# Attention and two feed-forward layers in one kernel: later first values, more buffers for queries and bias rows, a doubling copy in four pieces

## The chip, the cores and the metric

One core of a Trainium2 chip runs the whole program. The metric is the device time of one execution in microseconds (us). The engines named below are TensorE (PE: matmuls, with weight loads shown apart as PEld), VectorE (DVE), ScalarE (ACT), GpSimd (POOL) and SyncE (SP), whose queue issues nearly all DMA transfers of this kernel.

## The reference

Attention over 2 batches, 8 heads, 576 positions and head size 64, with a bias that a tiny network makes from the distance of the two positions; then two feed-forward layers of 1152 tokens, 512 wide, 2048 hidden.

```python
scores = scale * np.matmul(q, k.transpose(0, 1, 3, 2))
x = (psi_rel / psi_i)[..., None]          # log1p(|i-j|) / log1p(max(i,1))
bias = np.maximum(x @ w1 + b1, 0.0) @ w2  # 32 hidden units, 8 heads; the same for both batches
attn = softmax(scores + bias.transpose(2, 0, 1)[None])
x = matmul(attn, v)                       # to (1152, 512)
x = prelu(x @ w_in, alpha) @ w_out        # layer 1
return rational(x @ w_in2) @ w_out2       # layer 2: a cubic over 1 + |b0 h| + |b1| h^2
```

## The kernel before

**Blocks and steps.** The queries are cut in nine blocks (`BLOCKS`, line 36): row blocks 0 to 3 of 128 queries for each of the two batches, and a last block that holds the remaining 64 queries of both batches. A block has four steps of two heads, 36 steps in all. A step n has scores (L332, PE), the row maximum with the bias added (L344, DVE, which writes p), the exponential (L355, ACT), the flip of p by matmuls with the identity (L365 and L369, PE), its copies out (L375 and L379 on DVE, L381 on ACT), and the values (L393, PE).

**Bias blocks.** Both batches use one bias tile `bias[j]` for each row block j. It is made in eight rows (four for the last). A row has four hidden tiles h (L256 on ACT, L258 on DVE), eight matmuls (L272), an eviction into a tile be (L291 or L284 on ACT, L293 or L286 on DVE) and a move, a DMA from be into every eighth partition of the bias tile (`bias_move`, L298; L302 for the last block). The pool of be tiles has three buffers, so the eviction of row r waits until the move of row r-3 has landed. Row maxima of block 0 need all eight moves of bias block 0. The bias of the last block is made for 64 partitions, and `bias_again` (L306) copies it on DVE to the other 64, in two copies of four heads each.

**Loads.** SP issues, in order: the constants `sm`, the queries of block 0 (`load_q`, L219, 512 KB into a tile qraw), the keys by pairs of heads (`load_k`, L202, called K00 to K03 here for batch 0 and K10 to K13 for batch 1, 288 KB each), the second part of the table tt (L467), the values of a batch in five pieces (`load_v`, L213, 256 KB each). ACT casts a key tile (L206), DVE makes its low part (L210). The queries are cast on DVE (L237) and their low part made on POOL (L238, `split_q`). The pool `rq` has one qraw buffer: a load of queries waits until the last split of the block before is done. SP takes its instructions in order, so that what stands behind such a wait waits too.

**Order.** Nothing is scheduled by the compiler: `Agenda` (line 91) collects calls with a planned time and runs them sorted by it, so the numbers of table `Z` (line 72) set the order of each engine's instructions and nothing else. `warm` (L186) puts idle matmuls on PE at the start.

**After attention** come 96 up units (L686) and 96 down units (L701) of the feed-forward layers. Their weights are loaded by `unit_load` (L607, L609), and rebuilt on ACT (L617, L621), DVE (L625, L628, L650) and POOL (L655); the first of these run beside the last steps of attention, in the memory of the pools be, h and tt (`early_pools`).

Of the kernel before, what the change touches and what calls it, by code (L numbers as in the profile page):

```python
# [20 lines left out]
B, H, S, D = 2, 8, 576, 64  # L21
# [29 lines left out]
def row_tables():  # L51
# [36 lines left out]
}  # L88

# [16 lines left out]
def fused_kernel(ctx: ExitStack, tc: tile.TileContext, qT, q4T, kT, vp, m1_in, m1_out, m2_in, m2_out, small, ttab, out):  # L106
    nc = tc.nc
# [9 lines left out]
    ag = Agenda()  # L117
    pools = {}

    def open_pool(key, bufs, side, space=None):  # L120
        kw = {} if space is None else {"space": space}
        if space is not DRAM:
            kw["reuse_waits"] = "tile"
        cm = tc.tile_pool(name=key, bufs=bufs, side=side, **kw)
        pools[key] = (cm, cm.__enter__())
        return pools[key][1]
# [24 lines left out]
    pt_p = open_pool("pt", 2, "left")  # L151
    sm_p = open_pool("sm", 4, "left")
    xu_p = open_pool("xu", 1, "left")
    rq_p = open_pool("rq", 1, "left")
    q_p = open_pool("q", 8, "left")
    bb_p = open_pool("bb", 1, "left")
    ba_p = open_pool("ba", 1, "left")
    tt_p = open_pool("tt", 1, "right")
    h_p = open_pool("h", 10, "right")
    be_p = open_pool("be", 3, "right")  # L160
    ps_v = open_pool("ps_v", 1, "left", PSUM)
    ps_t = open_pool("ps_t", 2, "left", PSUM)
    ps_b = open_pool("ps_b", 1, "left", PSUM)
# [78 lines left out]
    bias, hid, bev, bps = {}, {}, {}, {}  # L242
# [60 lines left out]

    def bias_again(h):

        nc.vector.tensor_copy(out=bias[4][64:, h : h + 4], in_=bias[4][:64, h : h + 4])  # L306

    def bias_rows(j, r, at, step, at0, step0):
        z, z0 = step / 4.1, step0 / 4.1
# [166 lines left out]
    def step_time(n):  # L476
        t = T0
        for a, b, dt in ((0, 4, DT0), (4, 24, DT), (24, 32, DT2), (32, 99, DT3)):
            t += max(0, min(n, b) - a) * dt
        return t  # L480
# [12 lines left out]
    EARLY = rows[-1][2] + Z["bias_move"] * rows[-1][3] / 4.1 + 0.1  # L493
# [301 lines left out]
        nc.vector.memset(one, 1.0 + 1e-6)  # L795

    ag.at(step_time(20), moe_consts)
    ag.at(EARLY + 2.0, bias_again, 0)
    ag.at(EARLY + 4.0, bias_again, 4)
    ag.at(EARLY, early_pools)  # L800
    ag.at(M0 - 0.1, psum_u)
    ag.at(M1 - 0.1, late_psum)
# [123 lines left out]
```

## Time and profile before

| | us |
|---|---|
| median of 3 runs (lowest, highest) | 618.4 (617.63, 619.54) |
| the profiled execution | 615.66 |
| its span | 613.9 |
| PE busy | 595.5 (97%) |
| DVE busy | 519.8 (85%) |
| ACT busy | 436.6 (71%) |

The profiled execution is one more execution, with its own time: 1.76 us of it lie around the span. Times in the rows below are from the span's start. Busy time of PE says that matmuls were in it, not that they ran at the full clock; the granted clock is shown beside it as a share of 2.4 GHz.

### The profile page before, as it was taken

How to read it: one execution, taken by the hardware profiler on the slowest of the kernel's cores; microseconds unless marked ns; L12 is line 12 of the kernel's file. 1: busy time of each engine (PE TensorE's matmuls, PEld its weight loads, DVE VectorE, ACT ScalarE, POOL GpSimd, SP SyncE). 2: the span in 40 equal slices, each digit the busy share in tenths (PEclk: the TensorE clock that was granted, in tenths of full speed). 3: DMA queues.
4: the chain of work that ended last, by engine and by line, in shares of the span. 5: the costliest groups of instructions: out<-in, count | busy, mean ns of one | idle time of the engine just before them, and what ended most of it. 6: DMA issues, size and time to landing. Idle time of an engine off the chain costs nothing.

```text
span 613.9 us, 11091 instructions
## 1 busy us (share of the span) xinstructions
PE 595.5 (97%) x4278; PEld 522.0 (85%) x4278; DVE 519.8 (85%) x883; ACT 436.6 (71%) x724; POOL 77.1 (13%) x83
## 2 busy tenths in 40 slices
PE   8689999999999999999999999999999999999997
PEld 4456667767778999999999999998999999999985
DVE  6799898798688877779998787989999999789783
ACT  4789888889876555777766657787777887655660
POOL 1113222122235332000000020300000000000000
PEclk9889999999999999999999999999999999999999
DMA  9872444323553332445445557775200000001011
GB/s 248 187 198 76 117 118 119 97 72 94 151 152 104 94 113 105 137 130 157 156 146 168 172 167 234 204 253 188 87 1 0 1 2 0 2 0 52 1 52 52
DMA packets 41749, 67.62 MB, mean 110 GB/s; under 512 B 5040, under 2 KB 24800, under 8 KB 41696
## 3 DMA queue, kind: packets, MB, share of 16 engines
q1 hardware_dynamic: 41552, 66.57, 36.9%
q8 instruction: 33, 0.54, 0.4%
q10 hardware_dynamic: 144, 0.35, 0.2%
q14 instruction: 20, 0.16, 0.1%
HBM read 49.71 MB, written 6.58 MB: 92 GB/s over the span
## 4 chain that ended last, share of the span: by engine, by line
PE 78%; DVE 11%; DMA 5%; ACT 2%; issue 2%; POOL 0%; SPq 0%; DVEq 0%; ACTq 0%; POOLq 0%
PE ops L701 29%; PE hps L686 29%; PE bps L272 5%; PE pv L393 5%; PE s L332 4%; PE tp L369 4%; DMA bias<-be 2%; DMA qraw<-in_qT_dram 2%; DVE p L344 1%; DVE mid L625 1%; DVE h L258 1%; DVE w L655 1%; DVE ks L210 1%; DMA away<-mid 1%; DVE acc L773 1%
## 5 line engine op out<-in xcount | busy, mean ns | idle before, releaser
L686 PE MATMUL hps<-xh,w 128*128 128x384 f32 x768 | 204.0, 336 | 0.0
L686 PEld LDWEIGHTS hps<-xh,w 128*128 128x128 f32 x768 | 139.6, 188 | 1.1 <-issue 0.2
L686 PE MATMUL hps<-xl,w 128*128 128x384 f32 x384 | 128.7, 335 | 0.0
L701 PE MATMUL ops<-g,w 128*128 128x384 f32 x576 | 104.5, 336 | 0.0
L701 PE MATMUL ops<-w,g 128*128 128x512 f32 x432 | 102.5, 392 | 1.2 <-DVE acc L773 1.2
L701 PEld LDWEIGHTS ops<-g,w 128*128 128x128 f32 x576 | 100.8, 188 | 0.0
L701 PEld LDWEIGHTS ops<-w,g 128*128 128x128 f32 x432 | 80.7, 188 | 17.5 <-issue 1.5
L686 PEld LDWEIGHTS hps<-xl,w 128*128 128x128 f32 x384 | 72.1, 188 | 0.9
L756 ACT CAST g<-n 128x768 fp32r<-128x768 f32 x48 | 40.1, 835 | 40.0 <-DVE n L720 28.0
L355 ACT ACTIVATE p<-p,nm 128x576 f32<-128x576 f32 x72 | 55.7, 774 | 13.4 <-DVE nm L344 12.9
L272 PE MATMUL bps<-h,w2s 128*32 128x288 f32 x576 | 52.9, 432 | 8.9 <-DVE be L286 3.8
L625 DVE SCALAR_TENSOR_TENSOR mid<-mid,raw 128x512 int32<-128x512 int32 x64 | 48.9, 764 | 13.1 <-ACT mid L617 12.9
L258 DVE TENSOR_SCALAR h<-tt,sc,nb 128x576 f32<-128x576 f32 x98 | 55.8, 605 | 0.1
L344 DVE CUSTOM_DVE_ANT_0 p<-s,bias 128x576 f32<-128x576 f32 x72 | 52.3, 750 | 1.4 <-PE s L332 1.1
L761 DVE TENSOR_TENSOR g<-n,g 128x768 fp32r<-128x768 f32 x48 | 46.6, 970 | 7.8 <-ACT g L756 7.8
L332 PE MATMUL s<-ks,q 128*128 128x288 f32 x320 | 52.4, 308 | 0.6 <-DVE ks L210 0.6
L238 POOL TENSOR_TENSOR q<-qraw,q 128x256 fp32r<-128x256 f32 (+1 forms) x40 | 34.4, 859 | 144.2 <-DVE q L237 124.4
L628 DVE SCALAR_TENSOR_TENSOR mid<-raw,mid 128x512 int32<-128x512 int32 x64 | 49.5, 773 | 2.2
L369 PEld LDWEIGHTS tp<-ident,p 128*128 128x128 f32 x288 | 30.9, 141 | 23.5 <-issue 15.3
L393 PE MATMUL pv<-pt,v 128*64 128x128 f32 (+1 forms) x800 | 47.8, 267 | 0.2 <-DVE pt L375 0.2
L332 PEld LDWEIGHTS s<-ks,q 128*128 128x128 f32 x320 | 44.7, 192 | 2.6 <-issue 1.1
L369 PE MATMUL tp<-ident,p 128*128 128x128 f32 x288 | 46.6, 284 | 0.3 <-ACT pt L381 0.3
(77 smaller groups left out, 836.9 us busy)
## 6 DMA issues: line engine op xcount, KB each, us to landing
raw<-in_moe_w_in_dram SPq DMA_DIRECT2D x32, 512.0 KB, 4.3
raw<-in_moe_w_out_dram SPq DMA_DIRECT2D x32, 512.0 KB, 3.6
bias<-be SPq DMA_DIRECT2D x32, 288.0 KB, 4.8
qraw<-in_qT_dram SPq DMA_DIRECT2D x8, 512.0 KB, 5.5
away<-mid SPq DMA_DIRECT2D x16, 256.0 KB, 2.0
mid<-away SPq DMA_DIRECT2D x16, 256.0 KB, 3.9
v<-in_vp_dram SPq DMA_DIRECT2D x10, 256.0 KB, 7.5
kraw<-in_kT_dram SPq DMA_DIRECT2D x8, 288.0 KB, 5.0
```

Source lines behind the costliest of these rows:

```text
L258: nc.vector.tensor_scalar(out=h, in0=x, scalar1=sc[:, k : k + 1], scalar2=nb1, op0=ALU.mult, op1=ALU.max)
L272: nc.tensor.matmul(out=ps[32 * c : 32 * c + 32], lhsT=w2s, rhs=hid[j, r, c][:, u * HALF : (u + 1) * HALF], start=True, stop=True,)
L332: nc.tensor.matmul(out=ps[:, w, :HALF], lhsT=x[:, u, :], rhs=kk[:, h, w * HALF : (w + 1) * HALF], start=(i == 0), stop=(i == len(terms) - 1),)
L344: nc.vector.tensor_tensor_reduce(out=ptile[n][:, u, :].rearrange("p (w j) -> p w j", w=2), in0=pps.pop((n, u))[:, :, :HALF], in1=bias[j][: ...
L355: nc.scalar.activation(out=p, in_=p, func=AF.Exp, bias=nms.pop((n, u)), scale=-1.0, accum_out=sums[k][:, h : h + 1])
L369: nc.tensor.transpose(out=tp[:, j * P : (j + 1) * P], in_=p[:, u, o : o + P], identity=ident)
L393: nc.tensor.matmul(out=pv[64 * u : 64 * u + 64, hp, cols], lhsT=V[bb][:, j, h, :], rhs=pt[:, 4 * u + j if j < 4 else 8, cols], start=(j == ...
L625: nc.vector.scalar_tensor_tensor(out=m, in0=m, scalar=3, in1=raw[:, :, 0], op0=ALU.logical_shift_left, op1=ALU.bitwise_or)
L628: nc.vector.scalar_tensor_tensor(out=m, in0=raw[:, :, 1], scalar=-(2 ** 31), in1=m, op0=ALU.bitwise_and, op1=ALU.bitwise_or)
L686: nc.tensor.matmul(out=ps, lhsT=a, rhs=b, start=(i == 0), stop=(i == len(prs) - 1))
L701: nc.tensor.matmul(out=ops[ly, c, m], lhsT=a, rhs=b, start=(f == fs[0] and i == 0), stop=(f == fs[-1] and i == 2))
L761: nc.vector.tensor_tensor(out=gt[:, 1], in0=tmp.pop(p), in1=gt[:, 0].bitcast(F32), op=ALU.subtract)
```

## The change

The table of planned times: K02 and K03 are loaded at 9.5 and 11.2 instead of 3.0 and 3.2, the first values from 19.3 on instead of 4.0, and the next block's queries are loaded 2.6 after a block's first step instead of 5.34 (`loadq`).

```diff
-    "load_k00": 1.68, "load_k01": 1.9, "load_k02": 3.0, "load_k03": 3.2, "load_k10": 24.0,
+    "load_k00": 1.68, "load_k01": 1.9, "load_k02": 9.5, "load_k03": 11.2, "load_k10": 24.0,
...
-    rq_p = open_pool("rq", 1, "left")
+    rq_p = open_pool("rq", 2, "left")
...
-    be_p = open_pool("be", 3, "right")
+    be_p = open_pool("be", 4, "right")
...
     def bias_again(h):
 
-        nc.vector.tensor_copy(out=bias[4][64:, h : h + 4], in_=bias[4][:64, h : h + 4])
+        nc.vector.tensor_copy(out=bias[4][64:, h : h + 2], in_=bias[4][:64, h : h + 2])
...
-    ag.at(EARLY + 2.0, bias_again, 0)
-    ag.at(EARLY + 4.0, bias_again, 4)
+    for h in range(0, H, 2):
+        ag.at(step_time(29 + h // 2) + Z["again"], bias_again, h)
```

SP's queue at the program's start, before (kraw: keys, v_136: values of batch 0, bias<-be: the moves of the first bias block):

```order
L202 DMA kraw<-in_kT_dram 64x1152 x2
L467 DMA tt<-in_ttab_dram 128x472
L202 DMA kraw<-in_kT_dram 64x1152 x2
L213 DMA v_136<-in_vp_dram 128x512 x5
L298 DMA bias<-be 16x8x576 x8
L202 DMA kraw<-in_kT_dram 64x1152 x2
```

and the same place after the change:

```order
L202 DMA kraw<-in_kT_dram 64x1152 x2
L467 DMA tt<-in_ttab_dram 128x472
L298 DMA bias<-be 16x8x576 x2
L202 DMA kraw<-in_kT_dram 64x1152
L298 DMA bias<-be 16x8x576
L202 DMA kraw<-in_kT_dram 64x1152
L298 DMA bias<-be 16x8x576 x5
L213 DMA v_136<-in_vp_dram 128x512 x5
L202 DMA kraw<-in_kT_dram 64x1152
L219 DMA qraw<-in_qT_dram 128x1024
L202 DMA kraw<-in_kT_dram 64x1152
```

K02 and K03 now stand between the moves, and all five values behind the eighth; the queries of block 1 now go between K10 and K11.

DVE at steps 29 to 31, as the difference of the two (L306 is the doubling copy, L344 a row maximum, L237 a query cast):

```order
 L344 ISA nm 128x1
-L306 COPY bias<-bias 64x2304
-L237 CAST q<-qraw 128x256
-L306 COPY bias<-bias 64x2304
-L375 COPY pt<-tp 128x128
...
+L237 CAST q<-qraw 128x256
+L306 COPY bias<-bias 64x1152
 L379 COPY pt<-tp 128x512
 L375 COPY pt<-tp 128x128
```

The two long copies go; the first short one stands one step later, and the other three each a step further on, the last behind the row maxima of step 32.

## Rows read from the trace of the kernel before

**Rows 1.** The page: busy us of an engine, share of the span, instructions.
```profile
PE 595.5 (97%) x4278; PEld 522.0 (85%) x4278; DVE 519.8 (85%) x883; ACT 436.6 (71%) x724; POOL 77.1 (13%) x83
```
**Rows 2.** Busy us by engine in four stretches, granted clock, DMA share, GB/s.
```profile
30.00:38.00 8.00, 6.39 (x45) 3.94 (x45) 7.33 (x14) 5.94 (x12) 1.90 (x1) 0.79 0.56 145
80.00:160.00 80.00, 80.00 (x880) 56.97 (x880) 69.08 (x186) 69.61 (x146) 17.09 (x20) 1.00 0.40 108
170.00:175.00 5.00, 3.75 (x38) 2.93 (x38) 4.61 (x11) 2.24 (x5) 2.68 (x3) 1.00 0.19 64
175.50:190.30 14.80, 14.74 (x152) 12.85 (x151) 13.83 (x34) 11.93 (x26) 7.36 (x14) 1.00 0.51 143
```
**Rows 3.** Waits in the first 30 us: who waited for whom, total, times, longest.
```profile
ACT be L291 <- DMA bias<-be: 4.4, 1, 4.4
...
DVE be L293 <- DMA bias<-be: 3.8, 1, 3.8
...
PE bps L272 <- ACT be L291: 3.1, 1, 3.1
```
**Rows 4.** Timeline of SP's queue: start, us, issue, count.
```profile
4.68 4.85 SPq L213 DMA_DIRECT2D v<-in_vp_dram  x5
...
10.50 0.61 SPq L298 DMA_DIRECT2D bias<-be  x1
```
**Rows 5.** DMA issues of the first 30 us: count, KB, median us to landing.
```profile
bias<-be SPq DMA_DIRECT2D x8, 288.0 KB, 3.3
```
**Rows 6.** Stretches as in rows 2, where only keys, values, moves were on their way.
```profile
9.00:12.00 3.00, 2.95 (x33) 1.00 (x32) 3.00 (x7) 1.62 (x3) 0.00 (x0) 1.00 0.99 193
12.00:15.75 3.75, 3.51 (x36) 1.41 (x34) 3.46 (x8) 1.37 (x2) 0.00 (x0) 1.00 1.06 366
15.75:18.75 3.00, 0.17 (x3) 0.17 (x6) 0.00 (x0) 0.96 (x2) 0.00 (x0) 0.92 1.04 207
```
**Rows 7.** Timeline of DVE to the first row maximum; idle time before in brackets.
```profile
9.99 5.47 DVE L258 TENSOR_SCALAR h<-tt,sc,nb 128x576 f32<-128x576 f32 x11
...
20.01 3.51 DVE L258 TENSOR_SCALAR h<-tt,sc,nb 128x576 f32<-128x576 f32 x7
...
24.42 0.82 DVE L293 TENSOR_SCALAR be<-bps,cv 128x576 f32<-128x576 f32 x1 [0.70 <-PE bps L272]
25.27 2.65 DVE L210 TENSOR_TENSOR ks<-kraw,ks 64x1152 fp32r<-64x1152 f32 x2
...
28.14 1.48 DVE L258 TENSOR_SCALAR h<-tt,sc,nb 128x576 f32<-128x576 f32 x2
29.62 0.76 DVE L344 CUSTOM_DVE_ANT_0 p<-s,bias 128x576 f32<-128x576 f32 x1
```
**Rows 8.** Timeline of PE: the fifth bias row's matmuls, and the first values.
```profile
14.82 0.69 PE L272 MATMUL bps<-h,w2s 128*32 128x288 f32 x8
...
40.40 1.31 PE L393 MATMUL pv<-pt,v 128*64 128x128 f32 x20
```
**Rows 9.** Timeline of ACT: the first cast of batch 1's keys.
```profile
39.66 1.15 ACT L206 CAST ks<-kraw 64x1152 fp32r<-64x1152 f32 x1
```
**Rows 10.** Timeline near 66 us: DVE's cast of new queries, and PE's next wait.
```profile
66.10 0.29 DVE L237 CAST q<-qraw 128x256 fp32r<-128x256 f32 x1 [0.86 <-DMA qraw<-in_qT_dram]
...
66.88 0.69 PE L272 MATMUL bps<-h,w2s 128*32 128x288 f32 x8 [0.24 <-DVE be L286]
```
**Rows 11.** Timeline near the end of attention.
```profile
169.03 1.35 DVE L306 COPY bias<-bias 64x2304 f32<-64x2304 f32 x1 [0.62 <-DMA bias<-be]
...
174.50 0.33 PE L365 MATMUL tp<-ident,p 128*128 128x128 f32 x1 [1.02 <-ACT pt L381]
...
180.40 1.29 POOL L455 TENSOR_TENSOR xl<-xu,xh 128x512 fp32r<-128x512 f32 x1
...
180.69 1.53 DVE L650 CAST w<-mid 128x512 fp32r<-128x512 f32 x1
...
191.58 0.42 DVE L650 CAST w<-mid 128x512 fp32r<-128x512 f32 x1
```

4 rows, old and new, of the table Z are left out of this document.

## The prediction

> **What bounds the kernel now.** I read the page first: PE is busy for 97% of the span [rows 1], so time can only be won where PE has gaps, and the slices of the page put these in the first 70 us and near 170 us. The windows then say what limits each stretch. From 80 to 160 us PE is busy 80.00 of 80.00 us while DVE has some 11 us to spare [rows 2]: what happens there on DVE, ACT or in the queues costs nothing as long as it stays inside that slack, and a lead gained earlier is carried through. At 170 to 175 us PE is idle for 1.25 us [rows 2], of which the timeline shows 1.02 in one wait for ACT's copy out behind a late row maximum [rows 11]. After 200 us PE has the feed-forward layers alone, so the start and the end of attention move the finish one for one.
>
> At the start the list of waits names one event: ACT's eviction waited 4.4 us and DVE's 3.8 us for a move to land, and PE 3.1 us behind ACT [rows 3]. SP's timeline tells why. The five pieces of values were issued from 4.68 us on, the first move at 10.50 [rows 4], and what the queue has issued goes in order: the windows show keys on their way at 193 GB/s from 9 to 12 us, values at 366 from 12 to 15.75, and the first two moves at 207 from 15.75 to 18.75 [rows 6]. The rows of DVE give what follows: eleven h tiles end at 15.46, and after the wait its chain runs with only 0.70 us of idle time (for PE) to the first row maximum at 29.62 [rows 7].
>
> **The first values behind the moves, with four be buffers.** Removed: the values' 1.31 MB at 366 GB/s, 3.6 us ahead of the first move, and the two keys, 0.59 MB at 193, 3.1 us [rows 6]. Also the fifth eviction, not the fourth, is now the first that needs a move landed.
>
> What DVE could then do: PE has the fifth row's matmuls done at 14.82 + 0.69 = 15.51 [rows 8]. That eviction would start there instead of at 19.27 (15.46 and the 3.8 us of [rows 3]), 3.8 us earlier; without the 0.70 us for PE, whose chain loses its wait too, the eighth eviction would start at about 20.0, and the row maximum 29.62 - 24.42 = 5.2 us behind it [rows 7], at 25.2. That is 4.4 us earlier and the upper bound of this part.
>
> What the DMA can do: a lone move lands 3.3 us after issue [rows 5], so the first lands at 13.8, in time for 15.5. The others come as fast as the rows are made, one in about 1.4 to 1.9 us, and K02 and K03 are now among them. A move of 0.295 MB takes 1.43 us at 207 GB/s and a key 1.53 us at 193 [rows 6]. Ten transfers back to back: the fourth move lands at 13.8 + 3 x 1.43 + 2 x 1.53 = 21.1, the eighth at 21.1 + 4 x 1.43 = 26.9. The eighth eviction, which needs the fourth move's buffer, then starts at 21.1 and not 20.0; by DVE's chain the row maximum could start at 26.3, but needs the eighth move at 26.9. I take 26.9: a gain of 2.7 us. The lower bound is 20% slower transfers (13.1 us become 15.7, the eighth at 29.5): no gain in this part. I stay near the measured rates, since the moves and keys in the rows are the same instructions.
>
> From 30 to 66 us DVE sets the pace, with nearly every microsecond busy (7.33 of 8.00 at its start [rows 2]), and it issues the same list as before, so the 2.7 us are carried to PE's unbroken stretch.
>
> Cover for the moved loads: the values are through 3.6 us behind the eighth move, at 30.5, and the first values matmul, at 40.40 before, comes at 37.7 [rows 8]: 7 us to spare. Behind them K10 is through at 32.0; its cast, at 39.66 before [rows 9], comes at 37.0. Two keys and the queries of block 1 follow, and later moves stand behind these on SP, but their block is due only after 60 us. So I cost the late values at nothing; with that cover gone every microsecond of lateness would stop PE.
>
> **Two query buffers, loads at 2.6.** DVE waited 0.86 us for queries at 66 us and PE 0.24 us behind it [rows 10]. The wait goes, as the load no longer needs the last split. PE gets back only its 0.24 us. Elsewhere the query waits lie in stretches where PE is full, so nothing. The earlier load now stands ahead of the round trip of the inverse sums on SP; that trip is read by DVE several microseconds later and PE is full meanwhile. I cost it at nothing, at most the 11 us of DVE's slack hides it.
>
> **The doubling copies.** Two copies of 1.35 us each, with 0.62 us of waiting for the moves before the first, pushed the row maxima and made the 1.25 us of idle PE [rows 2, 11]. They go from there; four copies of half the size, some 0.70 us each, come. The first still lies before 175.5 us; three lie in the stretch 175.50 to 190.30, where DVE is busy 13.83 of 14.80 us and so has 0.97 us to give [rows 2]. Three copies are 2.1 us: DVE ends that stretch 2.1 - 0.97 = 1.1 us later against a start that is 1.25 us earlier. What is late next is thus the row maxima of the last block's steps. Gain 0.1 us; the bounds are 1.25 (all copies in gaps) and a loss worked out with the third rival.
>
> **Sum.** 2.7 + 0.24 + 0.1 = 3.0 us. Against the profiled execution: 615.66 becomes 612.7. That execution is 2.7 us under the median of the three runs, 618.4, and the prediction is for such a median: 618.4 - 3.0 = 615.4, or 0.5% less.
>
> **Rivals.** First, the DMA does not hold the moves back: the ten transfers overlap with the making of rows and the clock of DVE decides. For it: the first keys go while the fourth row is made. Against it: rows 6 show the transfers at these rates with the engines full. It gives 4.4 + 0.24, with up to 1.25 at the end 5.9 us: 612.5. (The page "DMA: Bandwidth & Descriptors" of the Trainium skill, section Specifications, has a ceiling of 435 GB/s towards SBUF, by which a move would take about 0.7 us, an estimate from that page, and this rival would hold; the trace has 207 GB/s and does not agree for moves of this shape.)
>
> Second, the stall comes back as a slow clock. PE runs out of work while the first row maximum is awaited; in 30 to 38 us it had a mean granted clock of 0.79, between its two levels of 1.2 and 2.4 GHz, after such a wait [rows 2]. Its keys and fifth to eighth bias rows now end earlier, so it may sit idle longer. If all of that stretch ran at 1.2 GHz, its 6.39 us would become 6.39 x 0.79 / 0.5 = 10.1; of the 3.7 us more, 1.6 fit in PE's idle time there, and 2.1 are lost. Then 1.0 us is left: 617.4. Against it: before, PE already lay idle 3.1 us at 15.5, and that goes.
>
> Third, and slower than before: the short copies meet POOL. When POOL was in a subtraction of 1.29 us from 180.40 to 181.69, DVE's cast of 180.69 took 1.53 us; the same cast took 0.42 at 191.58 [rows 11]. It ended about 0.4 us after POOL did. POOL is busy 7.36 of 14.80 us there [rows 2]. If each of the four copies waits out a whole subtraction, they cost 4 x (0.70 + 1.29) = 8.0 us; less 0.97 of slack and 1.25 of earlier start, the end of attention is 5.8 us later, and with the 2.9 gained before it the kernel is 2.8 us slower: 621.2. It turns to a loss when the copies' waits add up to more than 2.9 + 0.97 + 1.25 - 2.8 = 2.3 us, 0.6 each. Against it: only one of the copies follows a query cast that has just started POOL in that stretch. (The Trainium skill, "SBUF — State Buffer", section SBUF: two separate sides, says that VectorE and GpSimd share a port pair as an exclusive lock and the one that starts second waits for the whole instruction; the 1.53 us agree.)
>
> **How the numbers follow.** Forecast 0.58, with a range of its own of 613.6 to 616.8; first rival 0.17, second 0.17, third 0.08. A measurement of this kernel tells a change from none at about 0.3%, 1.9 us. Faster: nearly all of the forecast (0.54), the first rival and a little of the second (0.01): 0.72. Within 0.3%: the rest of both, 0.20. Slower: the third, 0.08. The range 612.3 to 618.5 takes in the first two rivals and the run-to-run spread of the median; the third lies outside.
>
> **What would show it.** Right: ACT's and DVE's waits for a move under 1.5 us in the first 30 us, the first row maximum near 26.9, waiting for the move and not for DVE; PE without a gap from about 63 us; the L393 matmuls of step 0 without a wait for values; 1.02 us of idle PE at 174 gone but DVE full to 190 and small PE waits near 188. First rival: row maximum near 25. Second: granted clock under 0.7 in the 8 us around it. Third: copies of over 1.5 us. The prediction is wrong if the shift at the first row maximum is not found again at 80 us, or if the end of attention gives back over 1 us.

## The result and the profile after

The change takes 612.88 us in the median of 4 executions (612.56 to 613.58), the kernel before, on the same chip, 618.97 (4 executions, 617.63 to 619.71): a ratio of 0.991 with an interval of 0.988 to 0.993. Timed once more, beside four of the experiments below, it is 612.96 (7 executions, 612.33 to 613.79) against 616.76 (13, 614.98 to 621.80), a ratio of 0.992 (0.989 to 0.995). So it is faster, by 3.8 to 6.1 us where 3.0 were forecast; 612.9 lies inside the range of 612.3 to 618.5, near its lower end, and below the 613.6 that the forecast alone would have allowed. The profiled execution of the change took 613.58 us, its span is 611.8; that is only 2.1 less than before. Profile and timing thus give different sizes, which is taken up further down.

The page's first part answers to [rows 1]; PE's share has not moved, since its busy time fell by 1.7 us where the span fell by 2.1:

```profile
PE 593.8 (97%) x4278; PEld 521.0 (85%) x4278; DVE 520.2 (85%) x885; ACT 437.0 (71%) x724; POOL 77.1 (13%) x83
```

DVE has two copies more. The waits of the first 30 us answer to [rows 3] (who waited for whom, total, times, longest):

```profile
DVE be L293 <- DMA bias<-be: 2.0, 1, 2.0
...
DVE p L344 <- DMA v<-in_vp_dram: 1.2, 1, 1.2
```

ACT no longer waits for a move. Two waits of DVE for moves are left. The second is a row maximum, which reads moves and no values; the profile names values, which were issued right behind the last move, but in the version with the values later (below) it names a move. SP's timeline (start, us, issue, count) answers to [rows 4], DVE's to [rows 7]. For DVE two more rows of before are needed, the first and the fifth eviction:

```profile
9.26 0.82 DVE L293 TENSOR_SCALAR be<-bps,cv 128x576 f32<-128x576 f32 x1
...
19.27 0.82 DVE L293 TENSOR_SCALAR be<-bps,cv 128x576 f32<-128x576 f32 x1 [3.81 <-DMA bias<-be]
```

After the change, SP and then DVE:

```profile
10.10 1.39 SPq L298 DMA_DIRECT2D bias<-be  x2
11.54 0.61 SPq L202 DMA_DIRECT2D kraw<-in_kT_dram  x1
12.64 0.54 SPq L298 DMA_DIRECT2D bias<-be  x1
13.22 0.60 SPq L202 DMA_DIRECT2D kraw<-in_kT_dram  x1
14.08 9.32 SPq L298 DMA_DIRECT2D bias<-be  x5
23.46 2.56 SPq L213 DMA_DIRECT2D v<-in_vp_dram  x5
```

```profile
9.26 0.82 DVE L293 TENSOR_SCALAR be<-bps,cv 128x576 f32<-128x576 f32 x1
9.98 5.48 DVE L258 TENSOR_SCALAR h<-tt,sc,nb 128x576 f32<-128x576 f32 x11
15.60 0.82 DVE L293 TENSOR_SCALAR be<-bps,cv 128x576 f32<-128x576 f32 x1
...
22.03 0.82 DVE L293 TENSOR_SCALAR be<-bps,cv 128x576 f32<-128x576 f32 x1 [1.98 <-DMA bias<-be]
...
28.38 0.76 DVE L344 CUSTOM_DVE_ANT_0 p<-s,bias 128x576 f32<-128x576 f32 x1 [1.18 <-DMA v<-in_vp_dram]
```

The fifth eviction starts at 15.60, where before it waited for a move until 19.27. The eighth waits 1.98 us for the fourth move (issued at 14.08, with two keys before it in the queue), and the first row maximum 1.18 us for the eighth move: it starts at 28.38, 1.24 us earlier than the 29.62 of [rows 7], and not 2.7. Then two pieces of PE's timeline, and windows with busy us by engine, granted clock, DMA share and GB/s (as [rows 2]):

```profile
24.38 1.29 PE L332 MATMUL s<-ks,q 128*128 128x288 f32 x8 [2.78 <-DVE ks L210]
...
30.30 1.19 PE L272 MATMUL bps<-h,w2s 128*32 128x288 f32 x8 [3.57 <-DVE be L286]
```

```profile
22.00:26.00 4.00, 1.62 (x12) 1.57 (x12) 3.93 (x5) 3.84 (x5) 0.12 (x1) 1.00 0.97 202
26.00:30.00 4.00, 0.73 (x9) 0.16 (x8) 2.82 (x7) 0.82 (x3) 0.88 (x1) 0.99 1.02 326
30.00:34.00 4.00, 3.70 (x24) 2.30 (x24) 3.85 (x7) 2.87 (x7) 1.90 (x1) 0.58 1.03 247
34.00:38.00 4.00, 3.94 (x37) 2.35 (x33) 3.64 (x7) 2.87 (x7) 0.00 (x0) 1.00 0.93 172
...
80.00:160.00 80.00, 80.00 (x889) 56.64 (x882) 68.22 (x185) 69.70 (x147) 17.84 (x21) 1.00 0.37 102
```

PE lies idle for 2.78 us until DVE has made the low part of a key, which stands behind the late eighth eviction, then for 3.57 us until DVE, done with the late row maximum, evicts the next bias row. In the 4 us after that its granted clock is 0.58, most of the time the lower of its two levels, 1.2 GHz. (Before, PE lay idle 3.07 us until 18.59, which is gone, and 2.06 in the place of the 3.57.) From 80 to 160 us PE is full, as before.

For all that follows two marks of the PE timeline are enough: the first scores of step 28, in the stretch where PE is full, and the first up matmul of the feed-forward layers. Before, then the change:

```profile
165.93 1.30 PE L332 MATMUL s<-ks,q 128*128 128x288 f32 x8
...
200.80 0.42 PE L686 MATMUL hps<-xh,w 128*128 128x384 f32 x1
```

```profile
164.22 1.31 PE L332 MATMUL s<-ks,q 128*128 128x288 f32 x8
...
199.10 0.42 PE L686 MATMUL hps<-xh,w 128*128 128x384 f32 x1
```

The lead is 1.24 us at the first row maximum, 1.71 at step 28 and 1.70 at the up matmul: what the start gave is carried on, and the end of attention (34.87 us from mark to mark before, 34.88 after) gives and takes nothing. From the up matmul to the end of the span it is 413.1 and 412.7 us.

### The profile page after: what moved, and what is told of

Its sections match the earlier page's. It is cut to its first block, busy times and chain, and to the rows that moved or that the text cites. A ratio compares the mean times of both kernels' runs of the same rounds, so it can differ in the third digit from the quotient of the medians.

```text
span 611.8 us, 11090 instructions
## 1 busy us (share of the span) xinstructions
PE 593.8 (97%) x4278; PEld 521.0 (85%) x4278; DVE 520.2 (85%) x885; ACT 437.0 (71%) x724; POOL 77.1 (13%) x83
## 4 chain that ended last, share of the span: by engine, by line
PE 80%; DVE 11%; DMA 4%; ACT 2%; issue 2%; SPq 0%; DVEq 0%; ACTq 0%
PE ops L701 29%; PE hps L686 29%; PE pv L393 6%; PE tp L369 5%; PE s L332 5%; PE bps L272 5%; DVE ks L210 1%; DVE h L258 1%; DMA bias<-be 1%; DVE p L344 1%; DVE mid L625 1%; DMA qraw<-in_qT_dram 1%; DVE w L655 1%; DMA away<-mid 1%; DMA v<-in_vp_dram 1%
## 5 line engine op out<-in xcount | busy, mean ns | idle before, releaser
L272 PE MATMUL bps<-h,w2s 128*32 128x288 f32 x576 | 51.3, 421 | 6.4 <-DVE be L286 5.1
L344 DVE CUSTOM_DVE_ANT_0 p<-s,bias 128x576 f32<-128x576 f32 x72 | 52.3, 751 | 2.8 <-PE s L332 1.3
```

Of the source, the lines that this page charges most:

```text
L272: nc.tensor.matmul(out=ps[32 * c : 32 * c + 32], lhsT=w2s, rhs=hid[j, r, c][:, u * HALF : (u + 1) * HALF], start=True, stop=True,)
L344: nc.vector.tensor_tensor_reduce(out=ptile[n][:, u, :].rearrange("p (w j) -> p w j", w=2), in0=pps.pop((n, u))[:, :, :HALF], in1=bias[j][: ...
```

## The experiments

One more event has to be known first: the first eviction of bias block 0 starts between 8.2 and 10.3 us after the span's start in the profiles, whatever the kernel. So the start of the first row maximum is also given relative to it: +20.4 before (29.62 - 9.26), +19.1 after (28.38 - 9.26).

**The kernel before, and the change, once more.** No edit.

> The kernel before, unchanged, for a second profile and for its spread. Measured so far: this change takes 5.8 us off (ratio 0.9906), but the two profiled executions differ by only 2.1 us (615.66 and 613.58), and the profiled one of before was 2 to 4 us quicker than all four timed ones. Theory A (the start): executions of before differ at the start, where a wait of 3 us cools PE; a second profile of 617 to 620 us shows the scores of steps 15 to 20 later by 2 to 4 us than in the first profile, with a lower granted clock between 15 and 45 us. Rival B (the end): the same lead up to 160 us, and the extra 2 to 4 us between 160 and 200. Rival C: spread evenly over the feed-forward layers. If the profile is again near 615.7, the three stay apart only by the clocks and times of the timed runs.

Measured: 616.40 us (12 executions), ratio 0.999 (0.997 to 1.000); row maximum at 29.14, +20.1; step 28 at 165.40. A second profile of the same program thus repeats the relative mark to 0.2 us and the other two to 0.5. It was again a quick execution, so it does not tell where the slower ones lose their time.

> The changed kernel, unchanged, on the same chip and in the same rounds as the three below. The kernel before had a median of 618.97 us over 4 runs beside its first timing and 616.77 over 29 runs since, so if the first four were on the high side the ratio here is 0.993 to 0.995 and not 0.9906; if the 5.8 us were real, 0.989 to 0.992.

Measured: 612.96, given above, 3.8 us under the kernel before and not 5.8; row maximum at 27.99, +18.7, after a wait of 0.53; yet step 28 came at 164.43, 0.21 us later than in the first profile. The windows of this profile say where 0.6 us went:

```profile
26.00:30.00 4.00, 2.12 (x17) 0.91 (x19) 3.47 (x9) 1.24 (x4) 0.99 (x1) 0.50 0.98 311
30.00:34.00 4.00, 4.00 (x24) 2.26 (x24) 3.46 (x6) 2.88 (x6) 1.90 (x1) 0.50 1.02 249
34.00:38.00 4.00, 4.00 (x33) 2.14 (x29) 3.43 (x6) 2.27 (x6) 0.00 (x0) 0.77 0.96 179
```

A clock of 0.50, 0.50 and 0.77 is the lower level for some 10 of these 12 us (4 + 4 + 4 x 0.23 / 0.5); in the first profile it was some 3.4 (4 x 0.42 / 0.5), and the earlier start is gone again. Here the clock was at the lower level before the second gap, from about 25.6 us on, behind a first gap of 2.98 us (2.78 in the first profile).

**The loads alone.** The kernel before with the three new load times.

```diff
-"load_k02": 3.0, "load_k03": 3.2, ... "load_v0": 4.0
+"load_k02": 9.5, "load_k03": 11.2, ... "load_v0": 19.3
```

> Before, with only the order of the first loads changed (values behind the moves, two keys among them): three be buffers, one query buffer, two long copies. Theory A: most of the gain is here: 2 to 4 us under before (ratio 0.9935 to 0.997); the fourth eviction needs the first move, landed at about 13.8, and waits about 0.5 us; the eighth needs the fifth move and waits about 1.5 us more than in the changed kernel. Rival B (the end of attention carries the gain): under 1 us (ratio above 0.998).

Measured: 614.87 (12), ratio 0.996 (0.994 to 0.998). ACT still waits 4.2 us for moves, DVE 3.5:

```profile
ACT be L291 <- DMA bias<-be: 4.2, 3, 2.6
...
DVE be L293 <- DMA bias<-be: 3.5, 1, 3.5
```

Row maximum at 28.62, +19.4. With three be tiles the later evictions take over the stall.

**The fourth be tile alone.** The kernel before with one number changed.

```diff
-    be_p = open_pool("be", 3, "right")
+    be_p = open_pool("be", 4, "right")
```

> Before, with only the fourth be buffer; values still ahead of the moves. The first move still lands near 17.7, so the fifth eviction (not the fourth) waits from 15.5 to about 17.8, and ACT's fourth not at all; the fourth move is issued near 14.3 instead of 18.6, so the back-to-back queue lands it at about 21.9 and the eighth eviction starts at 22 instead of 24.4. First row maximum near 27.7, 1.5 to 2 us earlier than in before; 614.8 to 615.8 us. Rival: the buffer only pays behind early moves; under 0.7 us gain.

Measured: 615.54 (12), ratio 0.9972 (0.9950 to 0.9995). DVE's timeline:

```profile
17.76 0.82 DVE L293 TENSOR_SCALAR be<-bps,cv 128x576 f32<-128x576 f32 x1 [2.64 <-DMA bias<-be]
...
28.64 0.76 DVE L344 CUSTOM_DVE_ANT_0 p<-s,bias 128x576 f32<-128x576 f32 x1
```

The fifth eviction still waits 2.64 us for the first move, which is behind the values, as expected. But the eighth starts at 23.46 and not at 22, after 1.26 us of waiting for PE, and the row maximum lies at +19.7; 1.5 to 2 us were expected from it. Against +20.1 to +20.4 before, the buffer gives 0.4 to 0.6, the loads 0.7 to 1.0, both 1.0 to 1.7 (the change): they add up. By the medians the two parts are worth 1.6 and 1.9 us, together 3.5, and 3.3 in the version with all but the queries: they add up too, but to about twice what the marks show, and where the rest is won stays open.

**All but the queries.** The change with `rq` at one buffer and `loadq` at 5.34.

> The change without its query part: one qraw buffer, queries loaded 5.34 after a block's first step. Prediction on record: 0.24 us of the gain, so the ratio to before within 0.001 of the change's 0.9906. Rival B: the query waits of before matter at the end (the queries of the last block came late, at 179.65), so 1 to 2 us of the gain are lost (ratio 0.992 to 0.994).

Measured: 613.50 (12, 612.73 to 617.92), ratio 0.996 (0.994 to 0.998). DVE's waits for queries from 60 to 200 us, in all 2.4 us, are back; the change has none. Both expectations gave a ratio (0.991, or 0.992 to 0.994) below the one measured; by the medians the version lies 0.5 us above the change, and its executions scatter up to 617.92 where those of the change end at 613.79.

**The queries alone.** The kernel before with those two numbers changed the other way.

> Before, with only the query part of the change: two qraw buffers, loads at 2.6. On record: 0.24 us. By the medians of the parts undone so far (613.50 without the queries, 612.96 with): 0.5 us, 616.2. Theory Q: the single buffer is what scatters the executions of before (615 to 621 us, with the profiled one always at the low end), since the kernels with two buffers lay within 2 us of each other and the two with one did not: then no execution here over 618 and a median of 615 to 616. Rival: scatter as before, and the two-buffer kernels were steady for another reason (the first wait for a move, which they all lack).

Measured: 615.54 (12, 614.88 to 616.51) against 617.17 (23, 615.37 to 622.37), ratio 0.997 (0.996 to 0.999). The forecast had 0.24 us for this part; the median gives 1.6. Its profile, at 615.45 us, has step 28 at 165.96, where before had 165.93. That is not to say that nothing was won, because its first row maximum came late:

```profile
30.59 0.76 DVE L344 CUSTOM_DVE_ANT_0 p<-s,bias 128x576 f32<-128x576 f32 x1
```

That is +21.9, and 1.0 to 1.5 us later than in the two profiles of before, though up to there the loads and moves are issued in the same order. The fifth eviction waited until 19.97 us for the second move (19.27 and 18.79 before), and the eighth 0.97 us for PE (0.70 and 0.72). From the row maximum to step 28 it is then 135.4 us, against 136.3 in both profiles of before: 0.9 us less, more than the forecast. Whether the query part won them or a late start was made up in slack, one profile does not tell. The spread changes too: a standard deviation of 0.52 us and nothing above 616.51, while a quarter of the executions of the kernel before, over all its timings, lie above 618 us.

**The long copies back.** The change with the old two copies.

```diff
-    for h in range(0, H, 2):
-        ag.at(step_time(29 + h // 2) + Z["again"], bias_again, h)
+    ag.at(EARLY + 2.0, bias_again, 0)
+    ag.at(EARLY + 4.0, bias_again, 4)
```

> The change with the two long doubling copies at their old places. Prediction on record: 0.1 us of the gain, so the same time as the change to 0.3 us, with a wait of PE near 172 back and the waits near 178 to 191 gone. Rival B: the short copies brought 1 to 2 us (ratio 0.992 to 0.994). Rival D: they cost time, since the lead of 3.5 us over before at step 30 is down to 2.1 at the end of attention: this kernel is 0.5 to 1.5 us faster than the change (ratio 0.988 to 0.990).

Measured: 612.99 (6), ratio 0.993 (0.991 to 0.996): by the medians the same as the change, 612.96 (the kernel before took 616.8 beside both), so that the four pieces are worth nothing. In its profile the wait of PE is back, and the end of attention takes 35.92 us instead of 34.88:

```profile
173.16 0.33 PE L365 MATMUL tp<-ident,p 128*128 128x128 f32 x1 [1.02 <-ACT pt L381]
...
170.00:175.00 5.00, 3.27 (x25) 2.61 (x21) 3.95 (x10) 3.23 (x8) 2.30 (x3) 0.85 0.71 217
175.00:180.00 5.00, 5.00 (x51) 4.19 (x50) 3.51 (x10) 3.44 (x8) 1.38 (x4) 0.81 0.24 71
```

The granted clock falls behind this wait, to 0.62 from 173 to 177.5 us, which neither profile of the kernel before shows there (1.00 from 165 to 200, with the same wait). This execution, 614.43 us, was the longest of the six. The kernel before has 34.87 us with the same copies. So the wait behind the long copies shows no cost in the medians, and 1 us in the one profile in which the clock falls behind it.

**Values later still.** The change with `"load_v0": 26.5` instead of 19.3, so that K10, the queries of block 1 and K11 stand between the last moves and the values.

> The change with the first values moved three transfers further back, behind K10, the queries of block 1 and K11. Theory F: what is behind the eighth move does not matter; it lands at about 28.3 as in the change, and the time is the same within 0.3%. Rival G: the eighth move, issued at 22.87, lands at 26 to 27 and the row maximum starts 1.2 us earlier, at the end of DVE's own chain (27.2).

Measured: 612.64 (6), ratio 0.991 (0.988 to 0.995). Row maximum at 26.92 after 0.60 us of waiting, now for the move; but the first eviction lay at 8.41, and +18.5 is 0.2 to 0.6 earlier than the change's two profiles, which differ by 0.45 themselves. So it is not seen that the values behind the moves hold the eighth one. What an empty queue behind it would do was not tried.

**Keys back to the front.** The change with K02 and K03 loaded ahead of all moves, as before.

```diff
-"load_k02": 9.5, "load_k03": 11.2
+"load_k02": 3.0, "load_k03": 3.2
```

> The change with keys K02 and K03 back ahead of the moves, where the queue has nothing to do from about 9 to 11 us; values still behind the moves. Theory F (ten transfers back to back, as on record): the fourth move lands near 18.5 instead of 21.9, DVE's wait of 2.0 us for it goes, the eighth eviction starts near 20.1, and the first row maximum at 25.2 to 26 instead of 28.4; 1 to 2.5 us faster than the change. Rival G (the eighth move is held by the values behind it, which is what the wait of 1.2 us is put down to): the row maximum comes only 2 us earlier, still after a wait for a landing. Rival H (DVE's lead at the start is eaten by PE's cold clock or by ACT before 66 us): row maximum 2 to 3 us earlier, the same total within 0.5 us.

Measured: 610.35 (6, 609.62 to 611.38), ratio 0.988 (0.985 to 0.991): 2.6 us better than the change, beside which it was timed, and no execution of the one reaches the other's. DVE's timeline has no wait for any move:

```profile
10.32 0.82 DVE L293 TENSOR_SCALAR be<-bps,cv 128x576 f32<-128x576 f32 x1
...
16.67 0.82 DVE L293 TENSOR_SCALAR be<-bps,cv 128x576 f32<-128x576 f32 x1
...
21.04 0.81 DVE L293 TENSOR_SCALAR be<-bps,cv 128x576 f32<-128x576 f32 x1
...
26.12 0.74 DVE L344 CUSTOM_DVE_ANT_0 p<-s,bias 128x576 f32<-128x576 f32 x1
```

Relative to the first eviction the row maximum comes at +15.8, 3.3 us earlier than in the change's first profile, and put on the 9.26 of the kernel before that gives 25.1: the 25.2 that the prediction had worked out as the bound by DVE's own chain. The clock after it:

```profile
26.00:30.00 4.00, 1.96 (x20) 1.34 (x24) 3.94 (x9) 4.00 (x8) 1.74 (x1) 1.00 0.97 299
30.00:34.00 4.00, 3.06 (x32) 1.72 (x32) 3.94 (x7) 2.18 (x5) 0.17 (x1) 1.00 1.02 234
34.00:38.00 4.00, 3.71 (x45) 2.35 (x44) 4.00 (x11) 3.70 (x6) 0.00 (x0) 1.00 1.03 197
```

PE's gap ahead of the first bias matmuls is 2.18 us here and the clock stays at 1.00. Step 28 and the up matmul:

```profile
161.49 1.30 PE L332 MATMUL s<-ks,q 128*128 128x288 f32 x8
...
196.45 0.42 PE L686 MATMUL hps<-xh,w 128*128 128x384 f32 x1
```

So the two keys between the moves cost the change 2.7 us at step 28. That is not the clock alone: the last version below has the same loads, its clock did fall, and its step 28 comes at 161.18.

**Doubling by DMA.** The change without the copies; the moves of the last block go to both halves, 16 instead of 8.

```diff
-                rows = bt[2 * r + i : 64 : 8].rearrange("p h j -> p (h j)")
-                nc.sync.dma_start(out=rows, in_=be[64 * i : 64 * i + 64])
+                for o in (0, 64):
+                    rows = bt[o + 2 * r + i : o + 64 : 8].rearrange("p h j -> p (h j)")
+                    nc.sync.dma_start(out=rows, in_=be[64 * i : 64 * i + 64])
```

> The change with the doubling copies gone: each move of the last bias block is made twice, to partitions 0 to 63 and 64 to 127, by eight more transfers of 144 KB (16 instead of 8), about 0.7 us each on a queue that is 40% busy there. If the short copies cost what the trace of the change suggests (PE idle 1.9 us between 175 and 195, DVE full), PE's idle time there falls to under 1 us and the kernel is 1 to 2 us faster than the change. Rival: DVE stays full with the weights' work and PE's waits stay; the same within 0.5 us. If the last moves land after 170, it is slower.

Measured: 612.38 (7, 611.04 to 615.29), ratio 0.992 (0.989 to 0.995). The end of attention takes 33.77 us instead of 34.88 (163.08 to 196.85), so in the profiles DVE's copies cost 1.1 us there, but the median is within 0.6 of the change.

**Keys early and doubling by DMA.** The edits of both at once.

> keys_early and dma_doubling together: keys K02 and K03 ahead of the moves, and the last bias block doubled by DMA instead of on DVE. keys_early has a median of 610.35 us, 2.6 under the change; dma_doubling 612.38, 0.6 under it, with the way from the scores of step 28 to the first up matmul 1.1 us shorter (33.8 against 34.9 us). If the two are independent: 609.2 to 609.8, ratio 0.985 to 0.988. Rival: the doubling's gain is in the noise of the clock, 610.0 to 610.7.

Measured: 611.54 (6), ratio 0.990 (0.987 to 0.993), in two groups: 608.25 and 608.59, with a granted clock over the whole span of 1.000 and 0.999, and 611.33 to 612.92, with 0.994 four times. The median lies above what either expectation gave, the lower group below. The profile, with a clock of 1.0, belongs to the lower group; of the upper one there is none, so that a fall of the clock makes the difference is likely and not shown.

**Keys early and copies a step earlier.** The version with early keys, and

```diff
-        ag.at(step_time(29 + h // 2) + Z["again"], bias_again, h)
+        ag.at(step_time(28 + h // 2) + Z["again"], bias_again, h)
```

> keys_early with each short copy one step earlier: the first then stands where the trace of the change has DVE idle for 1.04 us (from 166.9, before the copy out of step 28's flip), and one copy of 0.75 us leaves the full stretch behind 172. If that stretch is bound by DVE, the way from the scores of step 28 to the first up matmul is 0.5 to 0.8 us shorter than the 34.9 us of the change and keys_early, and the median about 609.7 (keys_early: 610.35). Rival: the moves of the last bias block land only near 167 and DVE waits for them: no gain, 610.3 or more.

Measured: 610.31 (5, 609.38 to 610.38), ratio 0.989 (0.988 to 0.991): no better than early keys alone. The end of attention takes 34.35 us, 0.6 less than with early keys alone; its first copy now waits 0.51 us for a move. The program up to 160 us is that of early keys, and so is PE's gap; the clock behind it is not:

```profile
27.23 1.19 PE L272 MATMUL bps<-h,w2s 128*32 128x288 f32 x8 [2.18 <-DVE be L286]
...
26.00:30.00 4.00, 2.77 (x15) 1.85 (x16) 3.94 (x9) 3.75 (x8) 1.90 (x1) 0.62 1.05 315
```

After the same gap of 2.18 us the clock was 1.00 in one profile and 0.62 in the other.

This version and the one with early keys, at 610.31 and 610.35, beat both kernels.

## Why the prediction was right in direction and where its sizes were not

**The first row maximum.** The mechanism is as predicted: no wait of ACT for a move is left, the fifth eviction starts at 15.60 (15.51 were worked out), DVE is ready for the eighth at 20.05 (20.0), and the DMA holds back the eighth eviction and the row maximum. The term that failed is "ten transfers back to back: the fourth move lands at ... 21.1, the eighth at ... 26.9". They released DVE at about 22.0 and 28.4: 0.9 and 1.5 us late, so 1.2 us instead of 2.7 were won at this point (1.0 to 1.7 by the relative marks). From 22.0 to 28.4 are 6.4 us for four moves, 1.6 each where 1.43 had been taken. The rate was not what failed: the windows have 199 to 207 GB/s from 14 to 26 us. What failed is "back to back". By 22.0 us the DMA had moved 2.28 MB since 9 us, but only 1.77 MB, four moves and two keys, stood in the queue up to and with the fourth move; by 28.4 it had moved 3.79 MB, and the ten transfers are 2.95. Transfers issued later had thus moved bytes before the fourth and the eighth move released DVE. What held these two so long no run here shows. The moved keys were in the sum with 2 x 1.53 = 3.1 us and were taken as given; with them back at the front 2.9 to 3.3 us are won by the relative mark, all of what was left down to DVE's own chain. The first rival, in which the DMA does not hold back, is thus false for the change and true as soon as the keys go first; the DMA then carries them while it has nothing else to do (in the change the windows have 0 GB/s from 9.0 to 10.5 us).

**The slow clock.** The second rival was half real. The stall did come back, as PE gaps of 2.78 and 3.57 us and a clock of 0.58 in the 4 us behind them. Its sign was a clock under 0.7 in the 8 us around the first row maximum: the first profile has 0.85 there (24.4 to 32.4 us), the second 0.60 (24 to 32), so it was seen in one of the two. And it was priced at 2.1 us, and between the two profiles of the change, with 3.4 and some 10 us at the lower level, lie only about 0.6 (0.39 earlier at the row maximum, 0.21 later at step 28). DVE is busy 3.85 of the 4 us from 30 to 34, so that PE's pace alone does not set the end of that stretch. At the end of attention with the long copies back, the execution with a fall of the clock took 1.0 us longer than the change.

**Carried through.** The shift is found again: 1.24 at the row maximum, 1.71 at step 28, 1.70 at the up matmul, 2.1 in the span. In the second profile of the change it is smaller at step 28, 1.0 to 1.5 us against the two profiles of before. That the late values cost nothing is shown too: the values matmul of step 0 starts at 39.02, without a wait for them, at 40.40 before.

**The copies.** 0.1 was forecast and 0.0 measured by the medians, and in the profile of the change by the mechanism given. The timeline of the end in the change, which answers to [rows 11]:

```profile
170.15 0.75 DVE L306 COPY bias<-bias 64x1152 f32<-64x1152 f32 x1
...
175.70 0.46 POOL L238 TENSOR_TENSOR q<-qraw,q 128x128 fp32r<-128x128 f32 x1 [3.95 <-DVE q L237]
...
175.79 1.23 DVE L306 COPY bias<-bias 64x1152 f32<-64x1152 f32 x1
176.37 0.96 POOL L238 TENSOR_TENSOR q<-qraw,q 128x128 fp32r<-128x128 f32 x1
...
177.40 0.66 PE L369 MATMUL tp<-ident,p 128*128 128x128 f32 x4 [0.41 <-DVE pt L375]
...
181.14 0.76 DVE L306 COPY bias<-bias 64x1152 f32<-64x1152 f32 x1
...
185.09 0.33 PE L365 MATMUL tp<-ident,p 128*128 128x128 f32 x1 [0.71 <-ACT pt L381]
...
185.80 0.76 DVE L306 COPY bias<-bias 64x1152 f32<-64x1152 f32 x1
...
190.71 0.33 PE L365 MATMUL tp<-ident,p 128*128 128x128 f32 x1 [0.76 <-ACT pt L381]
```

The 1.02 us of idle PE at 174 are gone, and 0.41, 0.71 and 0.76 us later on take their place, the small waits that were announced. Two of them name ACT, but DVE is what is late: it is busy 14.7 of the 15 us from 175 to 190, and ACT waits 8.0 us for its row maxima from 163 to 200. The third rival is false: of the four copies one, at 175.79, met a subtraction of POOL that had begun at 175.70 and ended at 176.16. It took 1.23 instead of 0.75 us, 0.48 more, where 2.3 would have been needed for a loss; the next subtraction began inside the copy, took 0.96 instead of 0.46 and ended 0.31 us after it. (The Trainium skill, "SBUF — State Buffer", section SBUF: two separate sides, has VectorE, in a two-port mode, and GpSimd exclude each other from a shared port pair for a whole instruction. The copy's duration agrees, 0.37 us of POOL's rest and its own 0.75; the subtraction's does roughly.) The rival's price was for subtractions of 1.29 us, those of the layers' input (L455); the one met was of queries and short. (The cast of [rows 11] ended 0.53 us after POOL did, not 0.4.)

**The queries.** 0.24 us was the size of PE's wait in one profile. By medians the part gives 0.5 (the change against all but the queries) to 1.6 (alone), and the one profile has 0.9 less behind the first row maximum: mis-sized. A profile near the fast end of the spread may not show what the part removes. In 73 executions of the kernel before, timed beside the experiments, from 614.98 to 622.37 us, the clock over the span falls as the time rises (correlation -0.66): its median is 0.993, and the six above 620 us have 0.987 to 0.991. With two query buffers alone, all 12 lie between 0.992 and 0.994. That fits late queries which stop PE long enough for the clock to fall in some executions. The other three versions with one query buffer scatter as well, with standard deviations of 1.5 to 1.7. It is argued and not shown: no profile of such an execution was had, the kernel before, run again, has a standard deviation of only 0.76 us in its 12 and 0.70 in the 8 beside the last version, and of the versions with two buffers the two with doubled moves have 1.5 and 2.0. A fall of the clock behind the long copies, seen once, and a late first row maximum, seen once, are rivals that no run separates from it.

**The total.** By the profiles the change gives 2.1 us of span, by the medians 3.8 to 6.1. Profiled executions of the kernel before (615.66 and 615.03) lie at the low end of its times, those of the change (613.58 and 613.79) at its high end. The forecast subtracted a gain worked out in a fast execution, 3.0, from a median of slower ones; it landed in the range because two errors met: too much for the row maximum (2.7 for 1.0 to 1.7) and too little for what the medians gain beyond the profiles. That the size came out inside the range is in this part luck. Nor is the base firm: its 618.4 is a median of three, and all later medians of the same kernel beside the experiments lie between 616.4 and 617.2, from which 3.0 less would be 613.4 to 614.2. How the rest of the gain divides stays open.

## What to carry to other kernels

When loads are moved out from between a transfer and its waiter, ask for each of them where the DMA is idle: loads that fit into an idle stretch ahead should stay there, and only those that don't fit should go behind. And where a kernel's times spread by more than the effect looked for, compare that spread with one profile before pricing a wait from it, because the profile may have caught an execution without the long waits.

## What was not expected of the hardware

The first eviction starts at 8.2 to 10.3 us after the span's start, from profile to profile, which moves all marks of the first 30 us by up to 2 us; a mark relative to it repeats to 0.2 us in two profiles of before and 0.45 us in two of the change, but came 1.5 us later in the queries alone, where the second move landed late with the same loads and moves ahead of it. The length of a PE gap did not settle the clock behind it: after the same gap of 2.18 us it was 1.00 in one profile and 0.62 in another, and one program ran 3 us apart with its clock over the span at 1.000 or 0.994. Moves alone and moves with keys among them ran at 199 to 207 GB/s, while the values reach 366 [rows 6], and a move could land well after the bytes that stood ahead of it had passed.
